# Attention memories with a head's keys and values side by side in the array, in a fused attention, Fourier-mixing and feed-forward kernel

## The chip, the cores and the metric

The kernel runs on one core of a Trainium2 chip. The metric is the device time of one execution in microseconds (us). The time before is the median of three runs. The profile is one execution, taken by the hardware profiler; its span runs from the first to the last instruction.

## What is computed

Inputs are q, k, v (8 batches, 8 heads, 576 tokens, 64 values a head), phi (32 logits a token and head) and two weight matrices. Cut to what matters:

```python
a   = softmax(phi)                       # over the 32 memories, per batch, head and token
k_m = einsum('bhsm,bhsd->bhmd', a, k)    # 32 memory keys per head
v_m = einsum('bhsm,bhsd->bhmd', a, v)    # 32 memory values per head
attn = softmax(q @ k_m.T / 8)            # 576 x 32 per head
x = attn @ v_m                           # heads side by side: 576 x 512 per batch
u = x + real(fft(fft(x, axis=1), axis=2))
out = u + relu(norm(u) @ w1) @ w2        # 512 -> 2048 -> 512
```

The change touches the two lines that make k_m and v_m, and the places that read v_m.

## The kernel before

Everything is float32 outside and is multiplied as pairs of 16-bit floats: a number is a high word and a low word, and a product is the sum of three matmuls (high by high, low by high, high by low). Tokens are reordered so that tiles of 128 tokens pair with their mirror images in the Fourier step.

Two kinds of work share TensorE. The feed-forward part goes over 18 chunks of two token tiles: `ffn1` (its matmuls show as line 309, because `groups()` issues them, output `ph`) and `ffn2` (line 900, output `po`). The attention and mixing part is the generator `background()`: batch by batch, and in a batch four pairs of heads. `advance()` draws it on in steps between the feed-forward steps, so that the tiles of u are ready before their chunk. Batches 0 and 1 (`NX = 2`) have float32 memories of their own (`memory_f32`, `next_memories`); batches 2 to 7 use `pair_memory`, so it runs 6 x 4 = 24 times. The order on each engine is fixed when the program is built, by the framework's scheduler with its own estimate of the times.

For one pair of heads `pair_memory` does this, in order. ScalarE squares keys, values and q for a scale (lines 513, 516), a matmul of three columns adds them up (line 521), VectorE makes scales from that (lines 270 to 281, 525). `kvs[0]` and `kvs[1]` are the high and low words of keys (w = 0) and values (w = 1), as five token tiles of 128 columns, one head's 64 beside the other's. ScalarE writes the high words (line 527). The low words of the keys are VectorE's (line 534, 640 wide); those of the values are GpSimd's (line 530), after a scaled copy by ScalarE (line 529). Then TensorE makes for the keys and again for the values 15 matmuls (lines 542 to 553): the 128 x 128 words of one token tile are the loaded weights, and 64 columns of softmax weights (32 per head, from the tile `et`: high and low words of two pairs) stream. The result in `pm` is 128 rows (two heads' 64 features) by 64 columns (two heads' 32 memories), of which only the blocks of a head with itself mean anything; the others are masked off by `mk` when VectorE takes them out of PSUM as `kmf` (line 555) and `vmf` (line 556). The masked keys become high and low words `km` (ScalarE line 565, VectorE line 566), and `pair_scores` multiplies q with them into `psc` (18 matmuls of 64 columns), reduces (line 597), and goes on to the softmax.

`values` scales `vmf` of all four pairs, splits it into words, has it transposed by DMA to `vbdt`, and multiplies it with the Fourier table `vt` into `pv` (line 680, 64 rows by 32 columns of the array). `mix_x` makes attn @ v_m from `vbdt` (output `px`, line 309, 128 columns). The table `vt` is loaded twice by `load_vt`: once early for batches 0 and 1, and once into `stg` for the rest. `mk` is one small load near the start.

Of the kernel before, what the change touches and what calls it, by code (L numbers as in the profile page):

```python
# [10 lines left out]
F32 = mybir.dt.float32  # L11
F16 = mybir.dt.float16
BF16 = mybir.dt.bfloat16
I32 = mybir.dt.int32
U32 = mybir.dt.uint32
AF = mybir.ActivationFunctionType
ALU = mybir.AluOpType
AX = mybir.AxisListType
# [23 lines left out]
NX = 2  # L42
# [55 lines left out]
def _constants():  # L98
    k = np.concatenate([TOK[0], TOK[2], TOK2[:33]])
    assert np.all(k % 2 == np.arange(NKC) % 2)  # L100
    ct = np.zeros((P, 2, 3, NKP), np.float16)

    def by_parity(w):
        return np.concatenate([w[:, 0::2], w[:, 1::2], np.zeros((w.shape[0], 1), np.float16)], axis=1)

    for cs, fn in ((0, np.cos), (1, np.sin)):
        for t, r in ((0, TOK[0]), (1, TOK2[:32])):
            v = fn(2 * np.pi * ((r[:, None] * k[None, :]) % S) / S) * 2.0**11
            if cs == 1:
                v[(r == 0)] = 0.0  # L110
                v[:, (k == 0) | (k == 288)] = 0.0
            hi, lo = (by_parity(w) for w in _split16(v))
            if t == 0:
                ct[:, cs, 0], ct[:, cs, 1] = hi, lo
            else:
                ct[0:32, cs, 2], ct[32:64, cs, 2], ct[64:96, cs, 2] = hi, hi, lo
        if cs == 0:
            odd = (np.where(k % 2 == 0, 0.0, -2.0) * 2.0**11).astype(np.float16)
            ct[96:98, cs, 2] = by_parity(np.stack([odd, odd]))
    j = np.arange(NJ)  # L120
    vt = np.zeros((P, NG, 2, DM), np.float16)
    f = SLOT.reshape(NG, P)
    for g in range(NG):
        ang = 2 * np.pi * ((f[g][:, None] * j[None, :]) % DM) / DM
        c = np.cos(ang) * 2.0**11
        s = np.sin(ang[:, 1:-1]) * 2.0**11
        vt[:, g, 0], vt[:, g, 1] = _split16(np.concatenate([c, s], axis=1))
    mk = np.zeros((P, 68), np.float32)
    mk[0:64, 0:32] = mk[64:128, 32:64] = 2.0**-EB
    mk[32:64, 64] = -1.0  # L130
    mk[97, 64] = -1.0
    mk[0:96, 65] = 1.0
    mk[:, 66] = np.where((np.arange(P) // 32) % 2 == 0, 1.0, -1.0)
    return ct, vt, mk
# [3 lines left out]
def kernel(  # L138
# [35 lines left out]
    un = const.tile([P, CH, DM], F32, name="un")  # L174
    ud = const.tile([P, 2, CH, DM], F16, name="ud")
    small = const.tile([P, 832], F32, name="small")
    mk = small[:, 0:68]
    ones = small[:, 68:132].bitcast(BF16)
    qsb = [small[:, 196 + i * 258 : 196 + i * 258 + NJ] for i in range(2)]
    half = small[:, 712:713]  # L180
    cout = small[:, 713:714]
# [17 lines left out]
    hring = const.tile([P, NW, 2, 4, P], F16, name="hring")  # L199

    nk = 2 * NST * P
    kvs = [stg[:, 2, i * nk : (i + 1) * nk].rearrange("p (t w c) -> p t w c", t=NST, w=2) for i in range(2)]
    qs = [stg[:, 2, 2 * nk + i * NQ : 2 * nk + (i + 1) * NQ] for i in range(2)]
    et32 = et.rearrange("p g l t c -> p (g l t c)").bitcast(F32).rearrange("p (g t c) -> p g t c", g=2, t=NST)

# [16 lines left out]
    nc.gpsimd.memset(half, -0.5)  # L222
    for t in qsb:
        nc.gpsimd.memset(t, 0.0)
    scratch = const.tile([P, 400], F32, name="scratch")
    share = const.tile([P, 2 * NJ], F32, name="share")

    def flat(t, names):
# [14 lines left out]
    def tiny(tag, n, bufs=2):  # L243
        if tag not in rings:
            rings[tag] = [taken[0], 0]
            taken[0] += n * bufs
        o, i = rings[tag]
        rings[tag][1] += 1
        o += i % bufs * n
        assert taken[0] <= 400, taken  # L250
        return scratch[:, o : o + n]

    def upper(src):
# [79 lines left out]
    def load_vt():  # L333

        v = stg[:, 1] if marks.get("vt") else hring.rearrange("p a l f c -> p (a l f c)")[:, : NG * 2 * DM]
        marks["vt"] = nc.sync.dma_start(out=v, in_=vt_d)
        return [v[:, g * 2 * DM : (g + 1) * 2 * DM] for g in range(NG)]

    def pooling_f32(b, pl, pf, rest):
# [164 lines left out]
    def pair_memory(b, g, r, vmf, ivs):  # L504

        n = f"{b}_{g}"
        kv = r[:, :KV].rearrange("p (t w c) -> p t w c", t=NST, w=2)
        q = r[:, KV:]
        if b < NX:
            return q, None, kept_memory(g, vmf), 1.0 / 8.0  # L510
        am = tiny("am", 3, 1)
        for w in range(2):
            nc.scalar.activation(
                kvs[0][:, :, w, :].bitcast(BF16), kv[:, :, w, :], AF.Square, accum_out=am[:, 1 + w : 2 + w]
            )
        nc.scalar.activation(
            kvs[1][:, 0:3].rearrange("p t w c -> p (t w c)").bitcast(BF16), q, AF.Square, accum_out=am[:, 0:1]
        )
        pm = psg.tile([P, 512], F32, tag="g", name=f"pm_{n}")
        mm = groups()  # L520
        mm(pm[:, 128:131], lhsT=ones, rhs=upper(am), start=True, stop=True)
        sc = tiny("sc", 3, 2)
        isc = tiny("isc", 3, 2)
        norm_scale(sc, isc, pm[:, 128:131], 3, 14, n)
        nc.vector.tensor_copy(out=ivs[:, g : g + 1], in_=isc[:, 2:3])
        for w in range(2):
            nc.scalar.activation(kvs[0][:, :, w, :], kv[:, :, w, :], AF.Copy, scale=sc[:, 1 + w : 2 + w])  # L527
            if w in KP:
                nc.scalar.activation(kv[:, :, w, :], kv[:, :, w, :], AF.Copy, scale=sc[:, 1 + w : 2 + w])  # L529
                nc.gpsimd.tensor_tensor(  # L530
                    out=kvs[1][:, :, w, :], in0=kv[:, :, w, :], in1=kvs[0][:, :, w, :], op=ALU.subtract
                )
            else:
                nc.vector.scalar_tensor_tensor(
                    out=kvs[1][:, :, w, :],
                    in0=kv[:, :, w, :],
                    scalar=sc[:, 1 + w : 2 + w],
                    in1=kvs[0][:, :, w, :],
                    op0=ALU.mult,
                    op1=ALU.subtract,  # L540
                )
        for w in range(2):
            i = 0
            for ka, kb in ((0, 0), (1, 0), (0, 1)):
                for t in range(NST):
                    mm(
                        pm[:, w * 64 : w * 64 + 64],
                        lhsT=kvs[ka][:, t, w, :],
                        rhs=et[:, g // 2, kb, t, 64 * (g % 2) : 64 * (g % 2) + 64],
                        start=(i == 0),  # L550
                        stop=(i == 3 * NST - 1),
                    )
                    i += 1
        kmf = tiny("kmf", 64, 2)
        nc.vector.tensor_tensor(out=kmf, in0=pm[:, 0:64], in1=mk[:, 0:64], op=ALU.mult)
        nc.vector.scalar_tensor_tensor(
            out=vmf[:, g],
            in0=pm[:, 64:128].unsqueeze(1).to_broadcast([P, 2, 64]),
            scalar=isc[:, 2:3],
            in1=mk[:, 0:64].unsqueeze(1).to_broadcast([P, 2, 64]),  # L560
            op0=ALU.mult,
            op1=ALU.mult,
        )
        km = tiny("km", 64).bitcast(F16).rearrange("p (l c) -> p l c", l=2)
        nc.scalar.copy(out=km[:, 0], in_=kmf)
        nc.vector.tensor_tensor(out=km[:, 1], in0=kmf, in1=km[:, 0], op=ALU.subtract)
        es = tiny("es", 1, 2)
        nc.vector.tensor_scalar(
            out=es, in0=isc[:, 0:1], scalar1=isc[:, 1:2], scalar2=1.0 / 8.0, op0=ALU.mult, op1=ALU.mult
        )  # L570
        return q, sc, km, es
# [71 lines left out]
    def values(b, vmf, ivs, ahl):  # L643
# [28 lines left out]
            transpose(vbdt, vbd, False, f"vbd_{b}")  # L672
        vt = vts[b // 2 > 0]

        pvs = [psg.tile([P, 512], F32, tag="g", name=f"pv_{b}_{kb}") for kb in range(2)]
        with tc.high_priority(-40) if b == 1 else nullcontext():
            for i, (va, ta) in enumerate(((0, 0), (1, 0), (0, 1))):
                for g in range(NG):
                    for h in range(2):
                        nc.tensor.matmul(  # L680
                            pvs[h][g * M : g * M + M, :],
                            lhsT=vms[h * 64 : h * 64 + 64, va, g, 0, h * M : h * M + M],
                            rhs=vt[g][h * 64 : h * 64 + 64, ta * DM : (ta + 1) * DM],
                            start=(i == 0),
                            stop=(i == 2),
                        )
# [38 lines left out]
    def mix_x(b, key, col, n, rows, attnT, vbd):  # L725
        px = psg.tile([P, 512], F32, tag="g", name=f"px_{b}_{key}")
        mm = groups()
        for g in range(NG):
            for l in range(2):
                mm(  # L730
                    px[rows, g * P : (g + 1) * P],
                    lhsT=attnT[:, g, col // P, col % P : col % P + n],
                    rhs=vbd[:, l, g, :],
                    start=(l == 0),
                    stop=(l == 1),
                )
        return px
# [662 lines left out]
```

## Time and profile before

| | us |
|---|---|
| median of three runs | 935.48 |
| lowest and highest | 934.89, 936.61 |
| span of the profiled execution | 933.5 |
| TensorE matmul busy | 922.6 (99%) |
| VectorE busy | 603.8 (65%) |
| ScalarE busy | 487.8 (52%) |
| GpSimd busy | 265.9 (28%) |

A matmul's busy time in the profile includes its way through the array, which the next one overlaps; what a matmul costs in a stream is the distance from its start to the next start. In a row of the timeline that merges n of them, that is the time to the start of the next row, divided by n. "PEld" is the loading of weights, which overlaps the matmuls.

### The profile page before, as it was taken

What the parts mean: (1) busy time and instruction counts of PE and PEld (TensorE: products, weight loads), DVE (VectorE), ACT (ScalarE), POOL (GpSimd) and SP (SyncE); (2) the same over time, 40 slices, a digit from 0 to 9 for tenths busy, and PEclk for the clock granted to TensorE, in tenths of its full rate; (3) what the DMA queues carried; (4) which work ended last, traced back from release to release, by engine and by line L of the source; (5) the groups of instructions that cost most, each with busy time, mean ns of one, the idle gap of its engine ahead of it and who ended that gap; (6) DMA issues with size and microseconds to landing.
All of it is one profiled execution on the core that took longest, in us unless ns stands there. A gap on an engine that the chain in (4) does not pass through costs nothing.

```text
span 933.5 us, 19693 instructions
## 1 busy us (share of the span) xinstructions
PE 922.6 (99%) x8036; PEld 685.3 (73%) x8036; DVE 603.8 (65%) x1399; ACT 487.8 (52%) x955; POOL 265.9 (28%) x298
## 2 busy tenths in 40 slices
PE   9999899999999999999999999999999999999998
PEld 8977577776776777766767677777677667678887
DVE  5979966676558766777434776576755766544554
ACT  5658768755356544655234654475555544533331
POOL 1305524232306413345030541333321421300000
PEclk9999999999999999999999999999999999999999
DMA  9958632542227322635021833175315252210001
GB/s 326 388 199 288 167 88 39 110 128 65 53 55 168 105 65 48 174 77 139 2 68 27 179 87 99 24 146 130 72 46 98 80 142 91 46 32 15 24 6 41
DMA packets 118410, 96.52 MB, mean 103 GB/s; under 512 B 100656, under 2 KB 100912, under 8 KB 116272
## 3 DMA queue, kind: packets, MB, share of 16 engines
q1 hardware_dynamic: 118320, 95.26, 37.8%
q8 instruction: 63, 1.03, 0.5%
q14 instruction: 27, 0.22, 0.1%
HBM read 62.35 MB, written 13.63 MB: 81 GB/s over the span
## 4 chain that ended last, share of the span: by engine, by line
PE 63%; DVE 5%; ACT 2%; DMA 1%; issue 1%; POOL 0%; ACTq 0%; POOLq 0%
PE ph L309 27%; PE po L900 22%; PE po L962 6%; PE pm L309 2%; PE pp_t L309 1%; PE px_t L309 1%; PE psc L309 1%; PE pa L707 1%; DMA kept_t<-ud 1%; DVE eo L629 1%; DVE hring L891 1%; DVE stg L583 0%; PE pp_t L750 0%; ACT stg L527 0%; PE pf L383 0%
## 5 line engine op out<-in xcount | busy, mean ns | idle before, releaser
L309 PE MATMUL ph<-unring,w1t 128*128 128x256 f16 x3264 | 389.3, 273 | 0.0
L309 PEld LDWEIGHTS <-w1t 128*128 128x128 f16 x3264 | 314.8, 98 | 58.7 <-issue 2.1
L900 PE MATMUL po<-w2s,hring 128*128 128x512 f16 x1344 | 313.1, 379 | 0.2 <-DVE uring L1007 0.2
L900 PEld LDWEIGHTS <-hring 128*128 128x128 f16 x1344 | 128.9, 98 | 129.3 <-issue 1.1
L891 DVE SCALAR_TENSOR_TENSOR hring<-ph,hring 128x512 f16<-128x512 f32 x112 | 76.2, 680 | 61.3 <-ACT hring L890 61.2
L890 ACT ACTIVATE hring<-ph 128x512 f16<-128x512 f32 x112 | 65.9, 588 | 76.2 <-PE ph L309 73.1
L810 POOL TENSOR_TENSOR scratch<-scratch,small 128x1 f32<-128x1 f32 x36 | 23.1, 643 | 211.4 <-DVE scratch L809 211.3
L613 POOL TENSOR_TENSOR aring<-aring,scratch 128x384 f32<-128x384 f32 x28 | 24.8, 885 | 141.7 <-DVE scratch L611 137.0
L309 PEld LDWEIGHTS <-stg 128*128 128x128 f16 x1152 | 44.6, 98 | 8.7 <-issue 1.0
L831 POOL TENSOR_TENSOR ud<-un,ud 128x1024 f16<-128x1024 f32 x17 | 37.4, 2200 | 31.0 <-ACT ud L830 31.0
L607 ACT ACTIVATE aring<-aring,scratch 128x384 f32<-128x384 f32 x24 | 14.6, 610 | 51.0 <-DVE aring L606 51.0
L530 POOL TENSOR_TENSOR stg<-rawt,stg 128x640 f16<-128x640 f32 x12 | 17.4, 1449 | 71.1 <-ACT rawt L529 71.1
L786 DVE SCALAR_TENSOR_TENSOR uring<-px_t,scratch,share 128x256 f32<-128x256 f32 (+1 forms) x80 | 34.2, 476 | 3.2 <-PE px_t L309 3.0
L632 ACT CAST aeo<-eo 128x384 f16<-128x384 f32 x30 | 15.4, 512 | 38.2 <-DVE eo L629 38.2
L984 POOL TENSOR_TENSOR uring<-uring,share 128x256 f32<-128x256 f32 x3 | 2.2, 729 | 109.6 <-ACT share L981 109.6
L634 DVE SCALAR_TENSOR_TENSOR aeo<-aeo,small,eo 128x128 f16<-128x128 f16 x30 | 26.2, 874 | 10.7 <-ACT aeo L632 10.7
L861 PE MATMUL po<-w2s,hring 128*128 128x512 f32 x64 | 30.8, 606 | 1.5 <-ACT hring L847 1.5
L621 POOL TENSOR_TENSOR ahring<-aring,ahring 128x320 f16<-128x320 f32 x29 | 25.6, 882 | 23.2 <-ACT ahring L620 23.2
L309 PE MATMUL pm<-et,stg 128*128 128x64 f16 (+1 forms) x740 | 32.2, 195 | 0.0
L597 DVE TENSOR_REDUCE scratch<-psc 128x12 f32<-128x384 f32 x32 | 17.5, 547 | 22.1 <-PE pm L309 16.3
L623 POOL TENSOR_TENSOR aring<-aring 128x128 f32<-128x128 f32 x56 | 31.1, 575 | 1.9
L804 ACT ACTIVATE un<-uring 128x512 f32<-128x512 f32 x32 | 19.9, 624 | 21.4 <-DVE ud L922 10.3
(313 smaller groups left out, 1535.0 us busy)
## 6 DMA issues: line engine op xcount, KB each, us to landing
out<-uring SPq DMA_DIRECT2D x35, 256.0 KB, 2.3
rawt<-in_raw SPq DMA_DIRECT2D x13, 640.0 KB, 5.8
stg<-in_raw SPq DMA_DIRECT2D x13, 640.0 KB, 5.1
stg<-in_w SPq DMA_DIRECT2D x7, 1024.0 KB, 5.8
rawt<-in_raw SPq DMA_DIRECT2D x15, 384.0 KB, 3.3
stg<-in_raw SPq DMA_DIRECT2D x15, 384.0 KB, 3.2
phs<-in_raw SPq DMA_DIRECT2D x28, 160.0 KB, 4.5
w2s<-in_w SPq DMA_DIRECT2D x4, 1024.0 KB, 10.6
```

What stands on the lines that cost most here:

```text
L309: m = nc.tensor.matmul(out, lhsT=lhsT, rhs=rhs, start=start, stop=stop)
L613: eng.tensor_tensor(out=a, in0=a, in1=sm.unsqueeze(2).to_broadcast([P, 12, M]), op=ALU.mult)
L621: nc.gpsimd.tensor_tensor(out=ahl[:, :, 64:128], in0=av[:, 0:5], in1=ahl[:, :, 0:64], op=ALU.subtract)
L623: eng.tensor_tensor(out=a2[:, i : i + 4], in0=a[:, 0:4], in1=a[:, 4:8], op=op)
L634: marks[f"s{b}_{g}"] = nc.vector.scalar_tensor_tensor(out=lo[:, :4], in0=hi[:, :4], scalar=mk[:, 64:65], in1=eov[:, :4], op0=ALU.mult, op1 ...
L786: nc.vector.scalar_tensor_tensor(out=u[rows, hs], in0=px[rows, hs], scalar=igx[rows], in1=tm[rows, w * NJ + half : w * NJ + half + 256], o ...
L831: marks[f"ul{c}"] = nc.gpsimd.tensor_tensor(out=ud[:, 1], in0=un, in1=ud[:, 0], op=ALU.subtract)
L861: nc.tensor.matmul(po[t], lhsT=h[:, f, t], rhs=w[:, f], start=(j == 0 and f == 0), stop=(j == NW - 1 and f == UB - 1),)
L890: marks["fa"] = nc.scalar.activation(h[:, 0], phv, AF.Relu)
L891: marks["fd"] = nc.vector.scalar_tensor_tensor(out=h[:, 1], in0=phv, scalar=0.0, in1=h[:, 0], op0=ALU.max, op1=ALU.subtract)
L900: nc.tensor.matmul(po[t], lhsT=hs[j][:, lh, f * 2 + t], rhs=w2s[:, j * UB + f, lw, :], start=(j == 0 and f == 0 and i == 0), stop=(j == NW ...
L962: m = nc.tensor.matmul(po[n], lhsT=h[:, la, a], rhs=b[lb], start=(j == 0 and i == 0 and n in ("p1", "p6", "p5", "p4")), stop=(j == NW - 1 ...
```

## The change

For batches 2 to 7 the two words' tiles `kvs` are ordered anew: for each token tile keys of head 0, values of head 0, values of head 1, keys of head 1. The 128 loaded columns are then one head's keys and values. That head's 32 softmax weights stream; for the high words of keys and values the high and the low words of the softmax weights stream in one matmul of 64 columns (two runs of 32, 640 elements apart in the tile), and for the low words the high words alone in one of 32 columns. Per head these are 5 + 5 matmuls, so 20 per pair in place of 30. The products with the softmax weights' low words land in columns of their own, and a new VectorE reduction adds the two parts of each head into a tile `both` of 64 columns, from which `kmf` and `vmf` are then made. The low words of the keys are made by two VectorE instructions, 320 wide, in place of one.

The values of a head now lie in the half of the rows in which they did not before. So `vmf` has a mask of its own (64 more columns of `mk`), the second load of `vt` swaps its two halves of 64 rows and becomes two loads, `values` takes the other half of the rows for a head, and `mix_x` reads the two 64-column halves of `vbdt` in reverse order.

```diff
-    kvs = [stg[...].rearrange("p (t w c) -> p t w c", t=NST, w=2) for i in range(2)]
+    kvs = [stg[...].rearrange("p (t a c) -> p t a c", t=NST, a=4) for i in range(2)]
+    def of_kind(t, w):
+        return t[:, :, 1:3] if w else t[:, :, 0::3]
...
     def load_vt():
-        marks["vt"] = nc.sync.dma_start(out=v, in_=vt_d)
+        if marks.get("vt"):
+            for o in (0, 64):
+                nc.sync.dma_start(out=v[64 - o : 128 - o], in_=vt_d[o : o + 64])
+        else:
+            marks["vt"] = nc.sync.dma_start(out=v, in_=vt_d)
...
+            hi, lo = of_kind(kvs[0], w), of_kind(kvs[1], w)
+            nc.scalar.activation(hi, kinds[w], AF.Copy, scale=sc[:, 1 + w : 2 + w])
...
-                nc.vector.scalar_tensor_tensor(out=kvs[1][:, :, w, :], in0=kv[:, :, w, :], ...)
+                for h in range(2):
+                    nc.vector.scalar_tensor_tensor(out=lo[:, :, h], in0=kinds[w][:, :, h], ...)
-        for w in range(2):
-            i = 0
-            for ka, kb in ((0, 0), (1, 0), (0, 1)):
-                for t in range(NST):
-                    mm(pm[:, w * 64 : w * 64 + 64], lhsT=kvs[ka][:, t, w, :],
-                       rhs=et[:, g // 2, kb, t, 64 * (g % 2) : 64 * (g % 2) + 64], ...)
+        for h in range(2):
+            e = et[:, g // 2, :, :, 64 * (g % 2) + M * h : 64 * (g % 2) + M * (h + 1)]
+            for i in range(2 * NST):
+                la, t = divmod(i, NST)
+                mm(pm[:, h * 64 : h * 64 + (1 if la else 2) * M], lhsT=kvs[la][:, t, 2 * h : 2 * h + 2],
+                   rhs=e[:, 0, t] if la else e[:, :, t], ...)
+        both = tiny("both", 64, 1)
+        nc.vector.tensor_reduce(out=both.rearrange("p (h m) -> p h m", h=2),
+            in_=pm[:, :128].rearrange("p (h l m) -> p h m l", h=2, l=2), axis=AX.X, op=ALU.add)
-        nc.vector.tensor_tensor(out=kmf, in0=pm[:, 0:64], in1=mk[:, 0:64], op=ALU.mult)
+        nc.vector.tensor_tensor(out=kmf, in0=both, in1=mk[:, 0:64], op=ALU.mult)
...
-            in0=pm[:, 64:128].unsqueeze(1).to_broadcast([P, 2, 64]),
+            in0=both.unsqueeze(1).to_broadcast([P, 2, 64]),
-            in1=mk[:, 0:64].unsqueeze(1).to_broadcast([P, 2, 64]),
+            in1=mk[:, 68:132].unsqueeze(1).to_broadcast([P, 2, 64]),
...
-                    rhs=vbd[:, l, g, :],
+                    rhs=vbd[:, l, g] if b < NX else vbd[:, l, g].rearrange("p (h c) -> p h c", h=2)[:, ::-1],
```

## Rows read from the trace of the kernel before

**Rows 1.** The page: busy time, share of the span, instructions of each engine
```profile
PE 922.6 (99%) x8036; PEld 685.3 (73%) x8036; DVE 603.8 (65%) x1399; ACT 487.8 (52%) x955; POOL 265.9 (28%) x298
```
**Rows 2.** Busy time by stretches: start:end length, busy (instructions), clock, DMA share
```profile
165.00:265.00 100.00, 100.00 (x920) 71.42 (x919) 62.98 (x135) 50.38 (x97) 29.31 (x32) 1.00 0.35 81
265.00:365.00 100.00, 99.42 (x903) 69.73 (x901) 70.82 (x160) 54.53 (x113) 37.45 (x40) 1.00 0.39 97
```
**Rows 3.** TensorE's waits from 150 us on: total us, times, longest
```profile
PE psc L309 <- DVE scratch L566: 0.8, 2, 0.6
PE pa L699 <- DVE aeo L634: 0.6, 1, 0.6
PE po L900 <- DVE uring L1007: 0.2, 1, 0.2
```
**Rows 4.** Groups of TensorE's instructions by shape: xcount | busy us, mean ns
```profile
L309 PE MATMUL pm<-et,stg 128*128 128x64 f16 x720 | 29.6, 193 | 0.0
```
**Rows 5.** Timeline of TensorE, a pair's memory and scores: start us, us, what, xcount
```profile
611.56 1.04 PE L309 MATMUL pm<-et,stg 128*128 128x64 f16 x30
612.44 1.68 PE L900 MATMUL po<-w2s,hring 128*128 128x512 f16 x7
...
617.00 0.70 PE L309 MATMUL psc<-scratch,stg 128*128 128x64 f16 x18
617.54 0.17 PE L309 MATMUL pm<-scratch,small 128*128 128x3 bf16 x1
617.57 0.81 PE L900 MATMUL po<-w2s,hring 128*128 128x512 f16 x3
```
**Rows 6.** Timeline of TensorE, a stretch of the mixing of batch 2
```profile
242.85 0.83 PE L309 MATMUL px_t<-vbdt,attnT 128*128 128x128 f16 x12
243.52 0.71 PE L309 MATMUL ph<-unring,w1t 128*128 128x256 f16 x5
```
**Rows 7.** Timeline of the other engines around the pair of rows 5
```profile
607.59 0.89 DVE L534 SCALAR_TENSOR_TENSOR stg<-rawt,scratch,stg 128x640 f16<-128x640 f32 x1
...
609.90 1.51 POOL L530 TENSOR_TENSOR stg<-rawt,stg 128x640 f16<-128x640 f32 x1 [8.47 <-ACT rawt L529]
...
614.74 0.23 DVE L566 TENSOR_TENSOR scratch<-scratch 128x64 f16<-128x64 f32 x1 [1.62 <-ACT scratch L565]
```
**Rows 8.** Timeline around the pair at 297 us, whose scores waited
```profile
297.41 0.22 PE L309 MATMUL psc<-scratch,stg 128*128 128x64 f16 x2
297.41 0.75 DVE L566 TENSOR_TENSOR scratch<-scratch 128x64 f16<-128x64 f32 x1
...
298.21 0.64 PE L309 MATMUL psc<-scratch,stg 128*128 128x64 f16 x16 [0.58 <-DVE scratch L566]
```
**Rows 9.** Timeline around the pair at 431 us, the shortest lead that did not wait
```profile
430.13 0.22 DVE L566 TENSOR_TENSOR scratch<-scratch 128x64 f16<-128x64 f32 x1
...
431.35 0.70 PE L309 MATMUL psc<-scratch,stg 128*128 128x64 f16 x18
```
**Rows 10.** Groups of VectorE's instructions by shape, 165 to 765 us
```profile
L786 DVE SCALAR_TENSOR_TENSOR uring<-px_t,scratch,share 128x256 f32<-128x256 f32 x40 | 16.9, 475 | 2.3 <-PE px_t L309 2.3
...
L566 DVE TENSOR_TENSOR scratch<-scratch 128x64 f16<-128x64 f32 x24 | 6.0, 250 | 16.7 <-ACT scratch L565 16.4
...
L555 DVE TENSOR_TENSOR scratch<-pm,small 128x64 f32<-128x64 f32 x24 | 5.2, 217 | 2.7 <-PE pm L309 2.6
...
L390 DVE TENSOR_REDUCE scratch<-pl 128x2 f32<-128x128 f32 x5 | 1.4, 282 | 0.8 <-PE pl L383 0.8
```
**Rows 11.** Two lines' own views: count, duration ns min/median/max, first and last start
```profile
L534 DVE SCALAR_TENSOR_TENSOR stg<-rawt,scratch,stg x12: 876/884/1657, 169.3 to 740.3; 128x640 f16<-128x640 f32 x12
...
L625 DVE TENSOR_TENSOR eo<-aring x23: 275/866/1472, 188.0 to 759.9; 128x128 f32<-128x128 f32 x23
```
**Rows 12.** SP's issues of the two loads that change: duration ns, start us
```profile
L336 SPq DMA_DIRECT2D stg<-in_vt x1: 333/333/333, 116.3 to 116.3; - x1
...
L1196 SPq DMA_DIRECT2D small<-in_mk x1: 525/525/525, 2.9 to 2.9; - x1
```

More of the change, by code (lines that the diff above doesn't have):

```diff
@@ L127, in _constants @@
         vt[:, g, 0], vt[:, g, 1] = _split16(np.concatenate([c, s], axis=1))
-    mk = np.zeros((P, 68), np.float32)
+    mk = np.zeros((P, 132), np.float32)
     mk[0:64, 0:32] = mk[64:128, 32:64] = 2.0**-EB
+    mk[0:64, 100:132] = mk[64:128, 68:100] = 2.0**-EB
     mk[32:64, 64] = -1.0
@@ L176 @@
     small = const.tile([P, 832], F32, name="small")
-    mk = small[:, 0:68]
-    ones = small[:, 68:132].bitcast(BF16)
+    mk = small[:, 0:132]
+    ones = small[:, 132:196].bitcast(BF16)
     qsb = [small[:, 196 + i * 258 : 196 + i * 258 + NJ] for i in range(2)]
@@ L201 @@
     nk = 2 * NST * P
-    kvs = [stg[:, 2, i * nk : (i + 1) * nk].rearrange("p (t w c) -> p t w c", t=NST, w=2) for i in range(2)]
+    kvs = [stg[:, 2, i * nk : (i + 1) * nk].rearrange("p (t a c) -> p t a c", t=NST, a=4) for i in range(2)]
+    def of_kind(t, w):
+        return t[:, :, 1:3] if w else t[:, :, 0::3]
     qs = [stg[:, 2, 2 * nk + i * NQ : 2 * nk + (i + 1) * NQ] for i in range(2)]
@@ L224 @@
         nc.gpsimd.memset(t, 0.0)
-    scratch = const.tile([P, 400], F32, name="scratch")
+    scratch = const.tile([P, 464], F32, name="scratch")
     share = const.tile([P, 2 * NJ], F32, name="share")
@@ L249, in tiny @@
         o += i % bufs * n
-        assert taken[0] <= 400, taken
+        assert taken[0] <= 464, taken
         return scratch[:, o : o + n]
@@ L511, in pair_memory @@
         am = tiny("am", 3, 1)
+        kinds = [kv[:, :, w].rearrange("p t (h c) -> p t h c", h=2) for w in range(2)]
         for w in range(2):
             nc.scalar.activation(
-                kvs[0][:, :, w, :].bitcast(BF16), kv[:, :, w, :], AF.Square, accum_out=am[:, 1 + w : 2 + w]
+                of_kind(kvs[0], w).bitcast(BF16), kinds[w], AF.Square, accum_out=am[:, 1 + w : 2 + w]
             )
         nc.scalar.activation(
-            kvs[1][:, 0:3].rearrange("p t w c -> p (t w c)").bitcast(BF16), q, AF.Square, accum_out=am[:, 0:1]
+            kvs[1][:, 0:3].rearrange("p t a c -> p (t a c)").bitcast(BF16), q, AF.Square, accum_out=am[:, 0:1]
         )
@@ L526, in pair_memory @@
         for w in range(2):
-            nc.scalar.activation(kvs[0][:, :, w, :], kv[:, :, w, :], AF.Copy, scale=sc[:, 1 + w : 2 + w])
+            hi, lo = of_kind(kvs[0], w), of_kind(kvs[1], w)
+            nc.scalar.activation(hi, kinds[w], AF.Copy, scale=sc[:, 1 + w : 2 + w])
             if w in KP:
-                nc.scalar.activation(kv[:, :, w, :], kv[:, :, w, :], AF.Copy, scale=sc[:, 1 + w : 2 + w])
-                nc.gpsimd.tensor_tensor(
-                    out=kvs[1][:, :, w, :], in0=kv[:, :, w, :], in1=kvs[0][:, :, w, :], op=ALU.subtract
-                )
[L533 to L541, printed above, removed]
@@ L542, in pair_memory @@
-        for w in range(2):
-            i = 0
-            for ka, kb in ((0, 0), (1, 0), (0, 1)):
-                for t in range(NST):
[L546 to L553, printed above, removed]
+                nc.scalar.activation(kinds[w], kinds[w], AF.Copy, scale=sc[:, 1 + w : 2 + w])
@@ new lines, in pair_memory @@
+                nc.gpsimd.tensor_tensor(out=lo, in0=kinds[w], in1=hi, op=ALU.subtract)
+            else:
+                for h in range(2):
+                    nc.vector.scalar_tensor_tensor(
+                        out=lo[:, :, h],
+                        in0=kinds[w][:, :, h],
+                        scalar=sc[:, 1 + w : 2 + w],
+                        in1=hi[:, :, h],
+                        op0=ALU.mult,
+                        op1=ALU.subtract,
+                    )
+        for h in range(2):
+            e = et[:, g // 2, :, :, 64 * (g % 2) + M * h : 64 * (g % 2) + M * (h + 1)]
+            for i in range(2 * NST):
+                la, t = divmod(i, NST)
+                mm(
+                    pm[:, h * 64 : h * 64 + (1 if la else 2) * M],
+                    lhsT=kvs[la][:, t, 2 * h : 2 * h + 2],
+                    rhs=e[:, 0, t] if la else e[:, :, t],
+                    start=(i == 0),
+                    stop=(i == 2 * NST - 1),
+                )
@@ L554, in pair_memory @@
+        both = tiny("both", 64, 1)
+        nc.vector.tensor_reduce(
+            out=both.rearrange("p (h m) -> p h m", h=2),
+            in_=pm[:, :128].rearrange("p (h l m) -> p h m l", h=2, l=2),
+            axis=AX.X,
+            op=ALU.add,
+        )
         kmf = tiny("kmf", 64, 2)
-        nc.vector.tensor_tensor(out=kmf, in0=pm[:, 0:64], in1=mk[:, 0:64], op=ALU.mult)
+        nc.vector.tensor_tensor(out=kmf, in0=both, in1=mk[:, 0:64], op=ALU.mult)
         nc.vector.scalar_tensor_tensor(
@@ L673, in values, with at_row @@
         vt = vts[b // 2 > 0]
+        def at_row(h):
+            o = 64 * (h if b < NX else 1 - h)
+            return slice(o, o + 64)
         pvs = [psg.tile([P, 512], F32, tag="g", name=f"pv_{b}_{kb}") for kb in range(2)]
@@ L681, in values @@
                             pvs[h][g * M : g * M + M, :],
-                            lhsT=vms[h * 64 : h * 64 + 64, va, g, 0, h * M : h * M + M],
-                            rhs=vt[g][h * 64 : h * 64 + 64, ta * DM : (ta + 1) * DM],
+                            lhsT=vms[at_row(h), va, g, 0, h * M : h * M + M],
+                            rhs=vt[g][at_row(h), ta * DM : (ta + 1) * DM],
                             start=(i == 0),
```

## The prediction, made before the changed kernel ran

> **What bounds the kernel now.** I read the busy shares first, then the stretches, TensorE's own waits, and last the distances between its matmuls. TensorE is busy for 99% of the span [rows 1]; that alone says little, because each matmul's row includes its way through the array. The stretches say more: from 165 us on, where batches 2 to 7 are made, TensorE is covered for 100.00 of 100 us in one stretch and 99.42 in the next, at the full granted clock (1.00, its 2.4 GHz level), while VectorE stands at 63 to 71 of 100 us and the others below that [rows 2]. TensorE's waits for another engine from 150 us to the end come to 0.8 + 0.6 + 0.2 = 1.6 us [rows 3]. So in this part the time is the sum of the distances between the starts of TensorE's matmuls, and whatever shortens that sum shortens the run, as long as no other engine becomes late. The chunks after the last batch are TensorE's too, but the change doesn't touch them; they only start earlier.
>
> The distances: 30 matmuls of `pm` start at 611.56 and the next thing at 612.44, so one costs 0.88 / 30 = 29.3 ns [rows 5]. It is this number, not the 193 ns of its row [rows 4], that a removed matmul gives back. For comparison, 128 columns cost (243.52 - 242.85) / 12 = 56 ns [rows 6], 64 columns in `psc` 0.54 / 18 = 30 ns, and the three columns of the scale sum 0.03 us to two decimals, between 20 and 40 ns [rows 5].
>
> **Matmuls removed.** 30 become 20 in each of 24 pairs: 240 of the 720 [rows 4] go. At 29.3 ns that is 7.03 us. All of it lies on the path, since nothing else in this part ends later than TensorE.
>
> **Matmuls made narrower.** Of the 480 left, 240 stream 32 columns where 64 were streamed. The trace has no such matmul. On a straight line through 64 and 128 columns (29.3 and 56 ns) it would cost 29.3 - 32 x 26.7 / 64 = 16 ns; the three-column matmul, which lies further down that line and doesn't get below 20 to 40 ns [rows 5], says that the line ends above that. The other bound is no gain, 29.3 ns. I take 27 ns, from the three-column row, which is nearest in kind (a full set of weights for few columns): 240 x 2.3 = 0.55 us, bounds 0 and 3.2 us.
>
> The Trainium skill, "TensorE: Matmul & The Clock Gate", section "Back-to-back issue gap", gives about 60 cycles for anything from 1 to 64 columns, a floor of some 25 ns. By it the narrowing gives nothing and a removed matmul is worth 25 ns: 240 x 25 = 6.0 us, an estimate from that page, in place of 7.6. The three-column row agrees that there is a floor; the 64-column rows lie 4 to 5 ns above it, so the floor is not what sets a 64-column matmul here.
>
> **Streams in two runs.** The 240 wide matmuls read two runs of 32 columns, and the `px` matmuls of batches 2 to 7 (240 of them: 5 tiles of 8 a batch) read their two halves in reverse. The `ph` matmuls already stream two runs of 128 columns with a gap, 256 columns in all; their distance isn't lengthened by it in any row I could find, so I take nothing. Bounds: nothing, and, as the worst I would think of, half of a 64-column matmul for each, 480 x 15 = 7.2 us.
>
> **VectorE: longer by half a microsecond per pair.** The reduction reads 128 columns of PSUM: like line 390, 282 ns [rows 10]. `kmf` takes its input from SBUF and not from PSUM, as line 566 does: 250 in place of 217 ns [rows 10], and `vmf` the like. Two instructions 320 wide in place of one 640 wide: line 534 takes 884 ns [rows 11] and one 256 wide 475 [rows 10], so a column costs (884 - 475) / 384 = 1.07 ns and an instruction 202 ns, which the split pays once more. Sum 282 + 33 + 33 + 202 = 0.55 us, in 24 pairs 13 us of VectorE. Hidden, because VectorE has some 30 of 100 us free [rows 2]; the split also lies ahead of a later one: in the pair shown the low keys end at 608.48 and GpSimd's low values, for which the matmuls wait as well, at 611.41 [rows 7]. Without that cover the split would cost 24 x 0.2 = 4.9 us, but GpSimd would have to be 3 us faster.
>
> **The chain to the scores: the added wait.** `psc` waits for `km`, `km` for `kmf`, and that now for the reduction: 282 + 33 = 0.31 us later after the last `pm` matmul. Behind the reduction on VectorE are queued `kmf`, `vmf` and the next relu eviction (line 891); behind a waiting `psc` on TensorE is everything. How much lead is there? In the pair shown `km` is ready at 614.97 and `psc` starts at 617.00, 2.0 us [rows 5, 7]. In two of the 24 pairs there is none: at 297 us the scores waited 0.58 us, there because line 566 took 0.75 us [rows 8], and once more in the next batch (two waits, 0.8 us together [rows 3]). The shortest lead that didn't wait is 431.35 - 430.35 = 1.0 us [rows 9]. So 0.31 us is covered in 22 pairs and bare in two: 0.6 us, bounds 0 (the order is made anew, and these two may fall elsewhere) and 7.4 us (all 24 bare).
>
> **Edits at nothing.** The second load of `vt` becomes two: one issue of 0.33 us more on SP at 116 us [rows 12], while its first reader, line 680 for batch 2, comes after that batch's four pairs, whose first split is at 169.3 us [rows 11]; queued behind it are output stores and transposes, late by 0.33 us once. `mk` at 2.9 us grows from 34 to 66 KB; its issue took 0.53 us [rows 12], once; 0.1 us either way. ScalarE's instructions keep their sizes. `pm` is let go after the 0.28 us reduction and not after `kmf` and `vmf`, which can only help.
>
> **Sum.** Against the profiled execution's own span of 933.5 us: -7.03 - 0.55 + 0.6 = -7.0, so a span of 926.5. The median of the runs lies 2.0 us above that span (935.48); I carry this over: 928.5 us.
>
> **Rivals.** (a) The order is made anew by a scheduler that estimates times, and the chain is longer, so scores stand too early in TensorE's order more often. If 6 to 12 pairs come to wait 0.3 to 0.4 us, 2 to 5 us come back: 930.5 to 933.5. For it: VectorE is at 71 of 100 us in the stretch where both waits are [rows 2, 8]. Against it: 22 leads of 1 us and more. (b) The streams in two runs cost what I set at nothing, 15 ns each: 7.2 us, no change, 935.7. Against it: the `ph` matmuls. (c) Slower: VectorE's new work stretches beside GpSimd's. `kmf` and `vmf` now read SBUF alone, not PSUM; line 625, which does that too, takes from 275 to 1472 ns, median 866 [rows 11], while `kmf` from PSUM had a mean of 217 [rows 10]. Two such instructions 0.6 us longer each, and the 0.31 us, make 1.5 us per pair. Against the leads of some 2 us that would still be hidden; if the new order also halves the leads to 1 us, 24 pairs wait 0.5 us, 12 us, less 7.6: 939.9. It decides where the mean wait per pair passes 7.6 / 24 = 0.32 us. Against it: line 566, which also goes from SBUF to SBUF at the same point of the chain, has a mean of 250 ns. (d) The narrow matmuls give nothing: 929.1, or (the straight line) all of it: 925.8. Both lie with the forecast.
>
> **How the numbers follow.** Forecast with (d): 0.66, its own range 925.5 to 930.5. (a) 0.17, (b) 0.08, (c) 0.06, and 0.03 for a gain beyond the line. The range from 925.0 to 932.5 holds the forecast and most of (a). A measurement of this kernel can tell some 0.2%, 1.9 us, from no change: under 933.6 is faster. Faster: 0.66 + 0.15 + 0.03 = 0.84; the same: 0.02 of (a), 0.06 of (b), 0.01 of (c): 0.09; slower: 0.07.
>
> **What would show it.** `pm` in 480 matmuls, 20 in about 0.57 us from start to next start; 32 columns at about 27 ns; `px` still at 56 ns; TensorE's waits from 150 us on at 1.5 to 3 us, the scores' at 1 to 2; VectorE's sum 13 us up at a share still under 70%; the last `ph` some 7 us earlier, and the work from there to the end as long as before. The prediction is wrong if TensorE's waits grow by more than 3 us, if `px` or the wide `pm` matmuls lengthen, or if the stretch before 160 us, which the change barely touches, moves by more than 1 us because the order was made anew.

## The result and the profile after

| kernel | median us | ratio to before, 95% interval | span of the profiled execution |
|---|---|---|---|
| before | 936.05 | | 933.5 |
| changed | 926.30 | 0.9896 (0.9882 to 0.9910) | 924.8 |

The change made the kernel 9.75 us faster by the medians, where 7.0 us were forecast; the time, 926.3 us, lies in the stated range of 925.0 to 932.5. The two spans differ by 8.7 us. The other 1.0 us is no work that the change removed: the profiled execution of the changed kernel took 926.57 us, 1.8 more than its span; the same 1.8 on the span of before make 935.3 us, less than the later median of 936.05. The execution of before that was profiled was one of its quicker ones. Now and then an execution took some 20 us longer, at a mean granted clock of 0.98; the medians count these, while the ratios, and what is said below of single executions, leave them out.

Busy time, share of the span and instructions of each engine, changed kernel, in answer to [rows 1]:

```profile
PE 914.6 (99%) x7796; PEld 678.1 (73%) x7796; DVE 611.0 (66%) x1447; ACT 484.4 (52%) x955; POOL 266.0 (29%) x298
```

240 matmuls fewer, 48 VectorE instructions more (24 reductions, 24 second halves of the keys' low words). By stretches, in answer to [rows 2] (start:end, length, busy time of PE, PEld, DVE, ACT, POOL with counts, clock, DMA):

```profile
165.00:265.00 100.00, 100.00 (x882) 70.21 (x880) 64.92 (x151) 50.56 (x103) 29.67 (x32) 1.00 0.33 81
265.00:365.00 100.00, 100.00 (x878) 69.94 (x876) 65.92 (x152) 53.06 (x109) 35.34 (x40) 1.00 0.39 97
```

In these stretches TensorE has no gap, at the full granted clock, and VectorE still has a third of its time free. TensorE's waits from 150 us on, in answer to [rows 3], are down to 0.7 us from 1.6:

```profile
PE po L920 <- DVE uring L1027: 0.4, 1, 0.4
PE psc L314 <- DVE scratch L582: 0.3, 1, 0.3
```

The memory matmuls by shape (xcount | busy us, mean ns), in answer to [rows 4]:

```profile
L314 PE MATMUL pm<-et,stg 128*128 128x64 f16 x240 | 14.7, 192 | 0.1
...
L314 PE MATMUL pm<-et,stg 128*128 128x32 f16 x240 | 13.2, 177 | 0.0
```

And on the timeline of TensorE, in answer to [rows 5, 6]; the row of 20 is a whole pair, wide and narrow matmuls merged under the first one's shape:

```profile
611.76 0.70 PE L314 MATMUL pm<-et,stg 128*128 128x64 f16 x20
612.30 4.75 PE L314 MATMUL ph<-unring,w1t 128*128 128x256 f16 x42
...
247.44 0.83 PE L314 MATMUL px_t<-vbdt,attnT 128*128 128x128 f16 x12
248.11 0.38 PE L314 MATMUL ph<-unring,w1t 128*128 128x256 f16 x2
```

A pair now costs TensorE 612.30 - 611.76 = 0.54 us from start to next start, where 30 matmuls took 0.88 us [rows 5]: 0.34 us less, times 24 pairs is 8.2 us. Added up in the trace over all pairs, the distances of the 720 matmuls were 20.96 us and those of the 480 are 13.15, which is 7.8 us less; in the changed kernel a wide matmul has a mean of 28.9 ns and a narrow one of 25.9. Reading the two halves of `vbdt` in reverse costs nothing: 0.67 / 12 = 56 ns as before [rows 6]. So 7.8 us of matmuls and 0.9 us of waits account for the 8.7 us between the spans. TensorE's waits before 150 us add up to 5.8 us in both, and the first matmul of `pair_memory` starts at 165.9 us where it started at 165.6: the part ahead of the change did not move.

### The profile page after: what moved, and what is told of

It reads as the page before. It is cut to its first block, busy times and chain, and to the rows that moved or that the text cites. A ratio compares the mean times of both kernels' runs of the same rounds, so it can differ in the third digit from the quotient of the medians.

```text
span 924.8 us, 19285 instructions
## 1 busy us (share of the span) xinstructions
PE 914.6 (99%) x7796; PEld 678.1 (73%) x7796; DVE 611.0 (66%) x1447; ACT 484.4 (52%) x955; POOL 266.0 (29%) x298
## 4 chain that ended last, share of the span: by engine, by line
PE 54%; DVE 2%; ACT 2%; issue 1%; DMA 1%; POOL 1%; POOLq 0%; ACTq 0%
PE ph L314 24%; PE po L920 19%; PE po L982 6%; PE pp_t L314 1%; PE px_t L314 1%; PE psc L314 1%; PE pm L314 1%; PE pa L727 1%; DMA et<-elt 1%; PE pp_t L770 0%; PE pv L700 0%; DVE eo L641 0%; DVE eo L645 0%; ACT stg L538 0%; ACT un L824 0%
## 5 line engine op out<-in xcount | busy, mean ns | idle before, releaser
L314 PEld LDWEIGHTS <-stg 128*128 128x128 f16 x912 | 35.9, 97 | 5.4 <-issue 1.0
L792 DVE SCALAR_TENSOR_TENSOR share<-pp_t,scratch,small 128x257 f32<-128x257 f32 (+1 forms) x48 | 21.0, 480 | 18.7 <-ACT small L789 18.4
L541 POOL TENSOR_TENSOR stg<-stg 128x640 f16<-128x640 f32 x12 | 19.1, 1594 | 47.2 <-ACT stg L540 47.1
L641 DVE TENSOR_TENSOR eo<-aring 128x128 f32<-128x128 f32 x29 | 26.6, 916 | 7.5 <-POOL aring L639 7.4
L864 PE MATMUL ph<-unring,w1t 128*128 128x256 f32 x128 | 30.8, 383 | 0.0
```

Source lines behind the costliest of these rows:

```text
L314: m = nc.tensor.matmul(out, lhsT=lhsT, rhs=rhs, start=start, stop=stop)
L541: nc.gpsimd.tensor_tensor(out=lo, in0=kinds[w], in1=hi, op=ALU.subtract)
L641: nc.vector.tensor_tensor(out=eo[:, 1:3, 0], in0=ap[:, 1:3, 0], in1=ap[:, 1:3, 1], op=ALU.add)
L864: nc.tensor.matmul(ph, lhsT=w[:, k, f * P : (f + 1) * P], rhs=unTs[0][:, k], start=(k == 0), stop=(k == NK - 1))
```

## Experiments

Theory A: from batch 2 on the time is the sum of the distances between TensorE's matmul starts, and VectorE's longer chain lies beside it. Rivals: the streamed columns, not the number of matmuls, set the cost; or (C) VectorE's chain to the scores is bare, and the change gains less than its matmuls give.

### The changed kernel again

> The changed kernel itself, so that the next three are compared with it on one chip. Theory A (the time from batch 2 on is the sum of the distances between TensorE's matmul starts): 926.3 us again, 9 to 10 us under the kernel before.

Measured: 926.91 us, ratio 0.9905 (0.9889 to 0.9920), span 925.3. The same as the first time, 0.6 us apart. The next three ran on the same chip.

### All matmuls 64 columns wide

```diff
-                    pm[:, h * 64 : h * 64 + (1 if la else 2) * M],
+                    pm[:, h * 64 : h * 64 + 2 * M],
...
-                    rhs=e[:, 0, t] if la else e[:, :, t],
+                    rhs=e[:, :, t],
```

> The changed kernel with 64 columns streamed in the low words' 240 matmuls too (it adds the products of low words by low words). Theory A, with 28.9 ns for 64 and 26.0 ns for 32 columns from the trace of the changed kernel: 240 x 2.9 ns = 0.7 us longer than the changed kernel, 927.0. Rival, narrowing gives nothing (a floor for both): the same, within 0.2 us. Rival, narrowing gives half of a stream (16 ns for 32 columns): 3 us longer.

Measured: 926.84 us, ratio 0.9910 (0.9896 to 0.9924), span 925.0. The times rule out the 3 us of the last rival, but can't tell 0.7 us from nothing. The trace can; TensorE's timeline for the pair above:

```profile
611.59 0.75 PE L314 MATMUL pm<-et,stg 128*128 128x64 f16 x20
612.17 4.75 PE L314 MATMUL ph<-unring,w1t 128*128 128x256 f16 x42
```

20 wide ones take 0.58 us, 29 ns each, against 0.54 us with ten of them narrow: 0.04 us a pair, 1.0 us in 24, and 0.8 us when all 480 distances are added up (13.97 us, where the changed kernel has 13.15). It is there, and was lost among the waits, which from 150 us on add up to 0.4 us in this profile and to 0.7 in the changed kernel's. Earlier, in the part that the edit doesn't touch, this profile has a stand of its own, after which the granted clock fell (columns of the second line as above):

```profile
105.23 3.20 PE L881 MATMUL po<-w2s,hring 128*128 128x512 f32 x4 [2.28 <-ACT hring L867]
106.00:109.00 3.00, 3.00 (x5) 1.34 (x5) 2.49 (x12) 2.97 (x7) 2.26 (x4) 0.50 0.64 199
```

That was made up for before batch 2: the first matmul of `pair_memory` starts at 165.9 us here too.

### Thirty narrow matmuls, with the reduction

```diff
-            for i in range(2 * NST):
-                la, t = divmod(i, NST)
+            for i, (la, le, t) in enumerate([(0, 0, t) for t in range(NST)] + [(1, 0, t) for t in range(NST)]
+                                            + [(0, 1, t) for t in range(NST)]):
+                o = h * 64 + le * M
...
+                    pm[:, o : o + M], lhsT=kvs[la][:, t, 2 * h : 2 * h + 2], rhs=e[:, le, t],
...
+                    start=(i in (0, 2 * NST)), stop=(i in (2 * NST - 1, 3 * NST - 1)),
```

> The changed kernel with the high words' matmuls split in two of 32 columns: 30 matmuls of 32 columns a pair in place of 10 of 64 and 10 of 32, the same columns streamed, reduction kept. Theory A (each matmul has a floor of 26 ns): 24 x (30 x 26.0 - 10 x 28.9 - 10 x 26.0) = 24 x 231 ns = 5.5 us longer than the changed kernel, 931.8. Rival, the streamed columns set the cost: no difference.

Measured: 932.91 us, ratio 0.9969 (0.9958 to 0.9980), span 931.1: 6.0 us over the changed kernel in the same session.

```profile
615.61 0.90 PE L314 MATMUL pm<-et,stg 128*128 128x32 f16 x30 [0.17 <-DMA et<-elt]
616.36 4.75 PE L314 MATMUL ph<-unring,w1t 128*128 128x256 f16 x42
```

0.75 us for 30, 25 ns each: 0.21 us a pair over 0.54, 5.0 us in 24. The rest of the 6 us is about the 1.0 us by which TensorE's waits in this profile (1.7 us) are above the changed kernel's. The streamed columns are the same, 960 a pair, and the time is not; the number of matmuls sets it. Each of these matmuls loads its own weights, so no run here tells the number of matmuls from the number of weight loads. "Side by side" alone, without streaming the two words as one, would have kept a third of the gain: 0.31% by the ratios, where the changed kernel has 0.95%.

### Thirty narrow matmuls, without the reduction

```diff
...
+                    pm[:, h * M : h * M + M], lhsT=kvs[la][:, t, 2 * h : 2 * h + 2], rhs=e[:, le, t],
+                    start=(i == 0), stop=(i == 3 * NST - 1),
...
-        both = tiny("both", 64, 1)
-        nc.vector.tensor_reduce(out=..., in_=..., axis=AX.X, op=ALU.add)
-        nc.vector.tensor_tensor(out=kmf, in0=both, in1=mk[:, 0:64], op=ALU.mult)
+        nc.vector.tensor_tensor(out=kmf, in0=pm[:, 0:64], in1=mk[:, 0:64], op=ALU.mult)
...
```

> As e2_thirty_reduced, but the three products accumulate in the same 32 columns of a head and the reduction is gone: keys and values side by side, nothing else. Theory A (the reduction lies beside TensorE's work and costs nothing): as e2 within 0.6 us, 931.8. Rival C (the reduction's 0.3 us in the chain to the scores is bare in every pair): 24 x 0.31 = 7 us under e2, 924.5.

Measured: 932.96 us, ratio 0.9970 (0.9958 to 0.9981), span 931.5. With and without the reduction the same time, to 0.05 us by the medians and 0.4 us by the spans. Rival C wanted 7 us between the two. The reduction, 283 ns in each of 24 chains, costs nothing that these two runs can tell. Their waits differ by more, and the other way: 2.4 us without the reduction, 1.7 with it.

### The reduction five times over

```diff
-        nc.vector.tensor_reduce(
+        for _ in range(5):
+          nc.vector.tensor_reduce(
```

> The changed kernel with the reduction done five times over into the same tile: 4 x 0.27 = 1.1 us more in the chain from the memories to the scores in each of 24 pairs, 26 us more of VectorE. Theory A (the chain has leads of 1 to 3 us, and the order is made with the longer chain in view): 0 to 3 us longer than the changed kernel. Rival C (the chain is bare): 24 x 1.1 = 26 us longer.

Measured: 928.62 us, ratio 0.9913 (0.9900 to 0.9927), span 926.8, that is 1.7 us by the medians and 1.5 us by the spans over the repetition of the changed kernel. That one ran earlier, beside other executions of before; by the two ratios it is 0.0008, 0.7 us, and their intervals overlap. The waits of TensorE from 150 us on:

```profile
PE psc L314 <- DVE scratch L583: 0.8, 2, 0.6
PE psc L314 <- ACT scratch L582: 0.4, 1, 0.4
PE pv L701 <- DVE share L684: 0.4, 1, 0.4
```

Each reduction takes 290 ns here, so every chain is 1.16 us longer, 28 us in all, and between 0.7 and 1.7 us of that come through, where rival C wanted 26. TensorE has other work to put ahead of the scores. The cover is not unlimited, it seems: three waits for the scores now, 1.2 us, where the changed kernel had one of 0.3.

### The split of the keys' low words alone, on the kernel before

```diff
-                nc.vector.scalar_tensor_tensor(out=kvs[1][:, :, w, :], in0=kv[:, :, w, :], ...)
+                for h in range(2):
+                    cols = slice(64 * h, 64 * h + 64)
+                    nc.vector.scalar_tensor_tensor(out=kvs[1][:, :, w, cols], in0=kv[:, :, w, cols], ...)
```

> The kernel before with only the keys' low words made by two VectorE instructions of 320 in place of one of 640. Theory A (it ends some 3 us before GpSimd's low words of the values): the same as the kernel before, within 1 us, with TensorE's waits moved a little by the new order. Rival: 24 x 0.2 = 4.9 us longer.

Measured: 939.08 us, ratio 1.0014 (1.0003 to 1.0024). The median says little here: five executions took 936.2 to 936.7 us and five 939.1 to 939.2, and nothing lies between. The expectation, within 1 us of the kernel before, held for the first five and failed for the others; the rival's 4.9 us came in none. The profiled one, span 937.3, is of the upper group. First its timeline around 290 us (all engines, what matters):

```profile
287.72 2.13 POOL L833 TENSOR_TENSOR ud<-un,ud 128x1024 f16<-128x1024 f32 x1 [4.16 <-ACT ud L832]
288.41 4.12 DVE L536 SCALAR_TENSOR_TENSOR stg<-stg,scratch 128x320 f16<-128x320 f32 x2 [2.26 <-ACT stg L527]
...
289.93 2.25 POOL L913 TENSOR_TENSOR un<-w2s 128x1024 f32<-128x1024 f16 x1
...
292.14 1.64 POOL L530 TENSOR_TENSOR stg<-stg 128x640 f16<-128x640 f32 x1
...
292.58 0.95 PE L309 MATMUL pm<-et,stg 128*128 128x64 f16 x15 [2.32 <-DVE stg L536]
```

then the same stretch by windows (columns as above):

```profile
291.00:292.50 1.50, 0.00 (x0) 0.00 (x0) 1.50 (x2) 0.62 (x2) 1.50 (x2) 1.00 1.06 203
293.00:296.00 3.00, 3.00 (x23) 2.20 (x21) 2.97 (x6) 0.83 (x2) 2.18 (x2) 0.50 0.34 55
```

In one pair of the 24 (batch 3, pair 1) the two halves took 4.12 us together, beside two of GpSimd's 2 us instructions; the median of a half is 0.55 us in this run, and in the kernel before the one instruction took 2.13 us in that pair. TensorE stood for 2.3 us; and after that stand its granted clock was 0.50, its 1.2 GHz level, for some 3 us. So on VectorE the split has a price where it falls beside GpSimd's long instructions.

That the lower group of executions is the one in which the clock didn't fall there is likely, but not shown: 3 us at half clock are 1.5 us of work and the groups are 2.5 apart, and no profile of the lower group was taken. The mean granted clocks on record agree, as far as they go: 0.996 to 0.998 in all five executions of the upper group; 1.000 in three of the lower, and 0.998 in two, in which it fell somewhere.

This run doesn't test what the prediction said of the changed kernel. Here the matmuls of the keys don't read the values' words: they go on at 292.58 (in the row of 15), before GpSimd has made the low values (292.14 + 1.64 = 293.78). In the changed kernel every matmul of low words reads both.

### The split in all pairs but that one

```diff
-                for h in range(2):
-                    cols = slice(64 * h, 64 * h + 64)
+                for h in range(2 - (n == "3_1")):
+                    cols = slice(0, P) if n == "3_1" else slice(64 * h, 64 * h + 64)
...
```

> As e5_split_alone, but in one of the 24 pairs (batch 3, pair 1, where TensorE waited 2.3 us for the second of the two instructions and its clock then fell) the keys' low words are made by one instruction again. Theory A' (the split is hidden in 23 pairs, and that pair made all of the 1 to 3 us): 936 us in all executions, within 0.5 us of the kernel before, no wait for line 536 over 0.5 us. Rival (the split costs something in many pairs, or the order moves the wait elsewhere): executions at 939 remain.

Measured: 936.61 us, ratio 1.0002 (0.9992 to 1.0012); the executions lie from 935.3 to 937.8 and none at 939. So the group at 939 is gone with the split of that one pair, and the split of the other 23 is free within some 0.1%. Two expectations failed: a wait for line 536 of 0.6 us is left, and the profiled execution took 937.8 us. The order was made anew, and other waits came to the same place. These are the longest; the 0.9, the 0.8 and the 0.6 us all lie between 280 and 300 us:

```profile
PE po L902 <- DVE uring L1009: 1.1, 2, 0.9
PE pm L309 <- POOL stg L530: 0.8, 1, 0.8
PE pm L309 <- DVE stg L536: 0.6, 1, 0.6
```

That is 2.3 us in all, as much as in the run before, with the pair's low keys made by one instruction. What differs in the profile is that TensorE stood three times and not once, and that the granted clock didn't fall (1.000 in the mean). So it isn't shown that the split made TensorE lose the 2.3 us; the two runs fit the reading that the group at 939 is the one in which the clock fell.

## Why the prediction was right, and where its terms were off

**What bounds the kernel: right.** The number of TensorE's matmuls, each at the distance read from the timeline, gave the sign and most of the size. The runs with thirty narrow matmuls show it from the other side.

**Matmuls removed and narrowed: right, the second term too small.** The prediction had 7.03 + 0.55 = 7.6 us; all pairs together give 7.8, and the one read above 8.2. The 240 removed are worth the 29.3 ns that were read. The narrow ones cost 25 to 26 ns, not the 27 that were taken from the three-column row of two decimals, so narrowing gives 0.8 to 1.0 us. The Trainium skill's floor of some 25 ns ("TensorE: Matmul & The Clock Gate", "Back-to-back issue gap") is what the narrow rows show, 0.75 us for 30. Its table puts 64 columns on that floor too; the row of 20 wide ones shows 29 ns, and so the estimate of 6.0 us worked out from that page was too low.

**Streams in two runs: right.** The wide `pm` matmuls, two runs of 32, stay at 29 ns, and `px` at 56 ns in reverse.

**VectorE's added work: hidden, as forecast.** The groups of VectorE's instructions in the changed kernel, 165 to 790 us, in answer to [rows 10]:

```profile
L544 DVE SCALAR_TENSOR_TENSOR stg<-rawt,scratch,stg 128x320 f16<-128x320 f32 x24 | 13.0, 579 | 0.8 <-ACT stg L538 0.6
...
L571 DVE TENSOR_TENSOR scratch<-scratch,small 128x64 f32<-128x64 f32 x24 | 8.8, 369 | 0.8
L572 DVE SCALAR_TENSOR_TENSOR vmf<-scratch,small 128x128 f32<-128x128 f32 x24 | 8.8, 365 | 0.0
...
L564 DVE TENSOR_REDUCE scratch<-pm 128x64 f32<-128x128 f32 x24 | 6.8, 283 | 3.9 <-PE pm L314 3.8
```

By these groups and those of before in the same stretch, the reductions (6.8 us), `kmf` (3.6 more), `vmf` (0.7 more) and the split (2.4 more) add up to 13.5 us, where 13 was forecast. VectorE's sum as a whole rose by only 7.2 us, from 603.8 to 611.0, because others of its instructions came out shorter in the new order. The reduction takes 283 ns where 282 was taken from line 390. `kmf`, now read from SBUF, has a mean of 369 where 250 was forecast and 217 was had. Its own view shows how:

```profile
L571 DVE TENSOR_TENSOR scratch<-scratch,small x24: 214/226/1859, 177.1 to 757.3; 128x64 f32<-128x64 f32 x24
```

and so does the timeline at the longest of them:

```profile
432.72 2.12 POOL L931 TENSOR_TENSOR un<-w2s 128x1024 f32<-128x1024 f16 x1
...
433.07 1.86 DVE L571 TENSOR_TENSOR scratch<-scratch,small 128x64 f32<-128x64 f32 x1
```

The median, 226 ns, is about the old one (214); single ones are stretched up to 1859. Five of the 24 run beside a GpSimd instruction, and these five are the ones over 300 ns. That is rival (c)'s mechanism, seen, but in too few pairs to bring back 0.32 us a pair. The Trainium skill ("GPSIMD Engine Reference", "1. Specifications") has GpSimd's SBUF interfaces shared with VectorE, with contention for VectorE instructions of two SBUF inputs. The trace fits it: `kmf` had one input in PSUM before and has both in SBUF now. The run with thirty plain matmuls bears it out: there `kmf` reads PSUM again, two of the 24 run beside a GpSimd instruction, and none is stretched:

```profile
L565 DVE TENSOR_TENSOR scratch<-pm,small x24: 205/215/228, 176.9 to 768.5; 128x64 f32<-128x64 f32 x24
```

No run takes GpSimd's instruction away.

**The added wait: wrong sign.** 0.6 us were added for two pairs without a lead; TensorE's waits fell by 0.9 us. The prediction carried the leads of the old order over to the new one, though it said that the order is made anew. What happened to the pair of [rows 8] can be read, from its keys' low words to its scores:

```profile
285.30 1.01 DVE L544 SCALAR_TENSOR_TENSOR stg<-stg,scratch 128x320 f16<-128x320 f32 x2
287.31 2.14 POOL L851 TENSOR_TENSOR ud<-un,ud 128x1024 f16<-128x1024 f32 x1 [2.78 <-ACT ud L850]
...
290.20 1.40 POOL L541 TENSOR_TENSOR stg<-stg 128x640 f16<-128x640 f32 x1
...
294.50 0.55 PE L314 MATMUL pm<-et,stg 128*128 128x32 f16 x15
...
298.61 0.69 DVE L582 TENSOR_TENSOR scratch<-scratch 128x64 f16<-128x64 f32 x1
...
300.43 0.70 PE L314 MATMUL psc<-scratch,stg 128*128 128x64 f16 x18
```

In the changed kernel both halves are done a microsecond before GpSimd's long instruction begins, and TensorE waits for nothing in that pair. The instruction that makes the low words of `km` is stretched as before (0.69 us where it was 0.75), but the scores stand 1.1 us behind its end, and so the 0.58 us of [rows 8] are gone. That the new order avoids the wait is not something the change does by design: the waits of TensorE from 150 us on add up to 1.6 us before, 0.7 changed, 0.4 all wide, 1.7 and 2.4 with thirty matmuls, 1.6 with five reductions, 3.3 and 3.4 with the split on the old order. Against the 1.6 us of before, an order made anew came out between 1.2 us better and 1.8 us worse, and the change drew a good one; that part of its gain is luck. Which of its edits moved the order was not tried.

**The split at nothing: right in the changed kernel, and for the reason given.** In its trace GpSimd's low words of the values, for which the same matmuls wait, end 2.2 to 5.5 us after the keys' in all 24 pairs; in the pair above at 291.60 and 286.31 us. The runs with the split on the kernel before don't speak against this, for there the keys' matmuls have no such cover.

**Edits at nothing** (the two loads of `vt`, the wider `mk`): no wait on TensorE names them. They were not tried alone.

**What made the forecast too long.** Of the 2.2 us between 928.5 and 926.3, the wait is 1.5, the narrow matmuls some 0.2, and the 2.0 us by which the median was put above the span, and which came to 1.5, the other 0.5.

## What to carry to other kernels

Where TensorE has no gaps, price a change by the distance from a matmul's start to the next start, read from a merged row of the timeline; many matmuls of few columns, each with weights of its own, are paid by their number, so put side by side what shares a stream and stream as one what shares weights. A longer chain on another engine is free as long as TensorE has other work to put ahead, and a test that multiplies the chain by five shows how much of it is covered. Where a scheduler makes the order anew, waits of single pairs are not carried over: give them a band (here 1.2 us less to 1.8 us more) and no sign.

## What the runs showed of the hardware that was not expected

- The distance between matmul starts with a full set of weights is 25 ns at 32 columns (0.75 us for 30), 29 at 64 (0.58 us for 20) and 56 at 128 (0.67 us for 12): from 64 to 32 columns it hardly falls.
- VectorE instructions with both inputs in SBUF were stretched beside GpSimd's: two of 320 columns took 4.12 us together where one has a median of 0.55, one of 64 columns 1859 ns where the median is 226. With the input in PSUM the latter kept to 205 to 228 ns. That they meet was to be expected; the size was not.
- After a stand of 2.3 us TensorE's granted clock was 0.50 for some 3 us, in two profiles (the split alone, and all wide at 103 us); with three stands in one place that add up to 2.3 us (all pairs but one) it stayed at 1.00. A short wait can cost more than its own length.
